# First pair's scores placed around the last group's values, and weight steps placed behind the pairs'

## The chip, the cores and the metric

The kernel runs on one core of a Trainium2 chip. That core has a matrix engine (TensorE, PE in the profile, with its weight loads shown apart as PEld), three element-wise engines (VectorE = DVE, ScalarE = ACT, GpSimd = POOL) and a sync engine (SP), which here issues nearly all transfers between HBM and the on-chip memory (SBUF). Products land in PSUM. Each engine takes its instructions in the order in which they were written and waits on semaphores for the others. The metric is the device time of one execution in microseconds, the median of several runs.

## What is computed

Three layers follow each other: attention over chunks of 32 queries with a local window and 8 memory keys, a gated two-layer network, and a second network with a softmax-like gate and a normalisation.

```python
# attention: B, H, S, D = 4, 8, 768, 64; per chunk of 32 queries a window of 56 keys and 8 memory keys
scores = scale * q_c @ k_full.T;  a = softmax(scores);  out_c = a @ v_full
# x: 3072 tokens x 512
a = x @ w_a;  b = x @ w_b                 # 512 -> 1536
x2 = (a * b) @ w_out                      # 1536 -> 512
h = x2 @ w_in;  solu = h * softmax(h)     # 512 -> 1024
out = (layernorm(solu) * g_ln) @ w_out2   # 1024 -> 512
```

The products are made in a 32-bit format that is rounded on writing, so each operand is kept as a high and a low part, and each product is three matrix products (low by high, high by low, high by high).

## The kernel before, in words

The 3072 tokens are six blocks of 512 tokens. A **group** is 128 queries of one batch entry with all eight heads; four groups make a block. A group passes through the stages P (score bank in PSUM, with masks), S (scores on PE), M (maximum and subtraction on DVE), X (exponential on ACT), N (sums, reciprocal, multiplication), T (transposes on PE, copied back by ACT), V (values on PE, high part cast by ACT) and L (low part on DVE).

Blocks 0 and 1 are done directly: for each of 12 slices f of the 1536 columns, PE makes the products with `w_a` and `w_b` (`ab`, lines 857 to 859, twelve products each, results in the PSUM banks ps0 and ps1, which exist once each); ACT copies the first to the tile G0 (line 1416); DVE multiplies it by the second (`gate`, line 872); ACT and DVE split the result (lines 874 and 878); and `x2_step` multiplies it by `w_out` one slice later. The groups of block 1 run between the products of block 0. A table gives the slot of the loop in which each of their stages is called. The last two of them, called i and j in the code, run after the loop of block 0, beside the first half of block 1's first slice.

The loop of block 1 is cut into 72 ticks, six per slice: half of the first product, the rest, half of the second, the rest, and two halves of the `x2_step` of the slice before. A table says what is called after each tick (`at(t, fn, ...)`); the call puts instructions at the end of the queues of PE, DVE, ACT and SP, whose order is the written one. Two kinds of work are placed there:

- **Pairs.** The groups of blocks 2 to 5 go through the stages two at a time (`pair_P` to `pair_V`, lines 296 to 373). During block 1 four pairs run, d = 4 to 7, one in each 16 ticks. Their queries and keys (640 KB per group) and values (512 KB per group) are loaded into the three buffers of the pool `ld`, in turn; a load waits until the buffer's reader three loads earlier is done.
- **Weight steps.** Blocks 2 to 5 use sums of weight quarters. For each slice q: `s1_whole` (DVE, line 488), `s1_sums` (four DVE operations, line 502), `s1_hi` (a cast on ACT, line 513, into one buffer h, the last third of the tile Z), and `s1_lo` (DVE, line 520); `s1_hi` and `s1_lo` each issue two stores of 256 KB (lines 507 and 508). There is one h: the cast of slice q+1 waits until the stores of slice q have read it. `wo_keep` of slice f issues two stores of 256 KB (line 474), a DVE sum (line 479) and one more store (line 480) of 256 KB.

The cast, the exponential and the copy after a transpose (`pair_T`, line 346) are all in ACT's one queue. The transposed scores stand in the tile EB, which `pair_V` (line 361) reads.

Of the kernel before, what the change touches and what calls it, by code (L numbers as in the profile page):

```python
# [48 lines left out]
NDIR = 2  # L49
# [6 lines left out]
def fused_kernel(  # L56
# [224 lines left out]

    def pair_load(d, i, values):

# [3 lines left out]
        if values:  # L287
            t = ld_tile(n - k, "v")
            nc.sync.dma_start(t, qkv[qi, :, k:n])
            quads[qi]["v"] = t.rearrange("k (c p d) -> k c p d", c=NCH, p=NP)  # L290
        else:
            t = ld_tile(k, "qk")
            nc.sync.dma_start(t, qkv[qi, :, 0:k])
            quads[qi] = dict(
                q=t[:, 0:q].rearrange("d (p t) -> d p t", p=NP),
                k=t[:, q:k].rearrange("d (p t) -> d p t", p=NP),
            )
# [13 lines left out]

    def pair_S(d):

        for i in range(2):
            qi = 2 * d + i
# [976 lines left out]
    for qi, at in zip(qs, (  # L1292
        (24, 24, "8a", "8a", "9b", 31, 32, 32),
        ("8a", 27, "9b", "9b", 31, 33, 34, 34),
# [19 lines left out]
    for f in range(NF1):  # L1314
# [25 lines left out]
        pend = (0, f, gh, gl)  # L1340
        run_slot()
    x2_step(*pend)
    i, j = qs[2:]
# [13 lines left out]
    att_L(i)  # L1357
    T(j)
    V(j)
    att_L(j)  # L1360

# [16 lines left out]
    def pair(d, places):  # L1378
        p, s, m, x, n, t, v = places
        for k, fn in zip(places, (pair_P, pair_S, pair_M, pair_X, pair_N, pair_T, pair_V)):  # L1380
            at(k, fn, d)
            if fn is pair_S:
# [6 lines left out]

    d0 = 2 * NDIR  # L1390
    for j in range(4):
        pair(d0 + j, [16 * j + k for k in (-2 if j else 0, 0, 1, 2, 3, 8, 10)])
    for n in ((0, False), (1, False), (0, True)):
        pair_load(d0, *n)
    for t, fn, i in ((41, x1_hi, 0), (44, x1_lo, 0), (46, x1_hi, 1), (48, x1_lo, 1)):
        at(t, fn, i)
    for q in range(NF1):
        for k, fn in zip(
            ((0, 2, 5, 7), (7, 8, 10, 12), (13, 14, 16, 19))[q % 3], (s1_whole, s1_sums, s1_hi, s1_lo)
        ):  # L1400
            at(16 * (q // 3) + k + 1, fn, q)
    for t, fn, i in (
# [5 lines left out]
    for f in range(NF1):  # L1408
        at((0, 0, 14, 14, 14, 32, 32, 44, 48, 52, 56, 60)[f], wo_keep, f)
    pend = None  # L1410
# [53 lines left out]
    for p, (a, b, c, d, e) in enumerate((  # L1464
# [420 lines left out]
```

## Time and profile before

| | |
|---|---|
| time, median of 3 runs | 889.62 us (889.38 to 890.72) |
| profiled execution: its time / its span | 891.03 us / 889.2 us |
| PE busy / DVE busy / ACT busy, share of the span | 97% / 81% / 45% |
| busy time of the DMA engines, queue of SP | 69.3% |

The span is the time from the first to the last recorded instruction; 1.8 us of the profiled execution lie around it. In a listing by time a row gives the start, the busy time, the engine, the line, the operation with output and inputs, and in brackets the idle time of that engine just before it and what ended it. [...]

### The profile page before, as it was taken

What the parts mean: (1) busy time and instruction counts of PE and PEld (TensorE: products, weight loads), DVE (VectorE), ACT (ScalarE), POOL (GpSimd) and SP (SyncE); (2) the same over time, 40 slices, a digit from 0 to 9 for tenths busy, and PEclk for the clock granted to TensorE, in tenths of its full rate; (3) what the DMA queues carried; (4) which work ended last, traced back from release to release, by engine and by line L of the source; (5) the groups of instructions that cost most, each with busy time, mean ns of one, the idle gap of its engine ahead of it and who ended that gap; (6) DMA issues with size and microseconds to landing.
All of it is one profiled execution on the core that took longest, in us unless ns stands there. A gap on an engine that the chain in (4) does not pass through costs nothing.

```text
span 889.2 us, 16756 instructions
## 1 busy us (share of the span) xinstructions
PE 860.2 (97%) x6696; PEld 709.9 (80%) x6696; DVE 717.3 (81%) x1162; ACT 398.1 (45%) x587; POOL 61.5 (7%) x77
## 2 busy tenths in 40 slices
PE   3899999999999999999999999999999999999998
PEld 3788877787888887888888888878888788888886
DVE  6999965978876675767967778998589999888882
ACT  3677643433343423334645544357254444444432
POOL 0000000000000000000000000000322223222110
PEclk9999999999999999999999999999999999999999
DMA  9995446987699888882798988558903555554353
GB/s 369 422 413 205 154 149 197 303 282 241 215 342 408 310 318 288 322 310 76 252 336 324 342 318 330 203 192 291 332 26 95 166 164 179 160 168 124 119 153 121
DMA packets 103215, 216.08 MB, mean 243 GB/s; under 512 B 8544, under 2 KB 64096, under 8 KB 97888
## 3 DMA queue, kind: packets, MB, share of 16 engines
q1 hardware_dynamic: 103104, 214.99, 69.3%
q8 instruction: 53, 0.87, 0.4%
q14 instruction: 26, 0.21, 0.1%
q0 software_dynamic: 32, 0.00, 0.0%
HBM read 147.85 MB, written 67.11 MB: 242 GB/s over the span
## 4 chain that ended last, share of the span: by engine, by line
PE 68%; DVE 15%; DMA 7%; issue 5%; ACT 2%; SPq 1%; POOL 1%; POOLq 0%; ACTq 0%; DVEq 0%
PE acc L756 24%; PE pab L1185 8%; PE acc L970 8%; PE pab L727 7%; PE acc L727 5%; PE pab L857 2%; PE pab L858 2%; PE pab L859 2%; DVE Z L407 2%; DVE Z L399 2%; PE px L361 2%; PE s L194 2%; PE px L259 1%; DMA r<-ztd 1%; PE acc L857 1%
## 5 line engine op out<-in xcount | busy, mean ns | idle before, releaser
L756 PE MATMUL acc<-w 128*128 128x512 f32 x978 | 227.5, 391 | 0.2 <-DMA w<-wsa 0.2
L756 PEld LDWEIGHTS acc<-w 128*128 128x128 f32 x978 | 182.8, 188 | 38.6 <-DMA w<-wsa 0.6
L1185 PE MATMUL pab<-w 128*128 128x512 f32 (+1 forms) x600 | 134.4, 381 | 1.1 <-ACT w L1157 1.1
L1185 PEld LDWEIGHTS pab<-w 128*128 128x128 f32 x600 | 109.4, 188 | 23.0 <-ACT w L1157 1.5
L857 PE MATMUL pab<-x,w 128*128 128x512 f32 (+1 forms) x200 | 79.2, 396 | 0.9 <-ACT x L273 0.9
L858 PE MATMUL pab<-x,w 128*128 128x512 f32 (+1 forms) x200 | 77.6, 388 | 0.1
L859 PE MATMUL pab<-x,w 128*128 128x512 f32 (+1 forms) x200 | 77.3, 387 | 0.0
L918 POOL TENSOR_TENSOR w2ld<-w2ld 128x256 f32<-128x256 f32 x44 | 37.9, 881 | 545.3 <-ACT r L747 497.1
L727 PE MATMUL pab<-w 128*128 128x512 f32 x288 | 70.3, 391 | 0.3 <-DMA w<-wos 0.3
L769 DVE TENSOR_TENSOR part<-acc,part 128x512 f32<-128x512 f32 x56 | 38.6, 689 | 34.8 <-PE acc L756 28.0
L727 PEld LDWEIGHTS pab<-w 128*128 128x128 f32 x288 | 53.7, 188 | 12.0 <-ACT w L698 0.7
L970 PE MATMUL acc<-w,hx 128*128 128x512 f32 x252 | 60.9, 391 | 1.4 <-ACT part L982 1.3
L970 PE MATMUL acc<-w 128*128 128x512 f32 x252 | 60.6, 391 | 0.1
L970 PEld LDWEIGHTS acc<-w,hx 128*128 128x128 f32 x252 | 47.1, 188 | 11.9 <-ACT part L982 1.7
L970 PEld LDWEIGHTS acc<-w 128*128 128x128 f32 x252 | 47.1, 188 | 10.2 <-ACT part L982 0.5
L727 PE MATMUL acc<-w 128*128 128x512 f32 x216 | 51.9, 390 | 0.1
L727 PEld LDWEIGHTS acc<-w 128*128 128x128 f32 x216 | 40.5, 188 | 8.8 <-ACT w L829 0.4
L857 PEld LDWEIGHTS pab<-x,w 128*128 128x128 f32 x200 | 38.4, 192 | 9.1 <-ACT x L273 1.2
L859 PEld LDWEIGHTS pab<-x,w 128*128 128x128 f32 x200 | 38.4, 192 | 7.5
L858 PEld LDWEIGHTS pab<-x,w 128*128 128x128 f32 x200 | 38.4, 192 | 7.4 <-DVE x L278 0.4
L702 DVE TENSOR_TENSOR w<-r,w 128x512 fp32r<-128x512 f32 x56 | 37.7, 688 | 1.9 <-ACT w L698 1.9
L857 PE MATMUL acc<-gh,w 128*128 128x512 f32 x96 | 38.1, 397 | 0.0
(236 smaller groups left out, 1403.6 us busy)
## 6 DMA issues: line engine op xcount, KB each, us to landing
w<-wsa SPq DMA_DIRECT2D x24, 1024.0 KB, 6.9
w<-wsb SPq DMA_DIRECT2D x24, 768.0 KB, 6.2
raw<-w1d_dram SPq DMA_DIRECT2D x11, 1536.0 KB, 21.7
qk<-qkv_dram SPq DMA_DIRECT2D x20, 640.0 KB, 6.3
w<-wos SPq DMA_DIRECT2D x48, 256.0 KB, 4.5
ztd<-r SPq DMA_DIRECT2D x84, 128.0 KB, 2.5
r<-ztd SPq DMA_DIRECT2D x21, 512.0 KB, 4.0
v<-qkv_dram SPq DMA_DIRECT2D x20, 512.0 KB, 4.9
```

The costliest lines, as they stand in the source:

```text
L194: nc.tensor.matmul(s[CQ * c:CQ * c + CQ, r, p, lo:hi], st["q"][rows, p, CQ * c:CQ * c + CQ], st["k"][rows, p, k0 + lo:k0 + hi], start=True ...
L361: nc.tensor.matmul(px[half:half + 64, r, p // 2, i, t], v[rows, c, p, :], at[rows, p, t], start=True, stop=True,)
L702: nc.vector.tensor_tensor(out=c[:, 1], in0=op_src(k), in1=c[:, 0].bitcast(F32), op=ALU.subtract)
L727: nc.tensor.matmul(ps, w[:, u, sl], g[:, v], start=first and n == 0, stop=last and n == 2, skip_group_check=True,)
L756: nc.tensor.matmul(ps, w[:, u, k], xx[v][:, k], start=(start and k == 0 and i == 0), stop=(stop and k == 1 and i == 2), skip_group_check=True,
L769: nc.vector.tensor_tensor(out=o, in0=a, in1=b, op=op)
L857: nc.tensor.matmul(ps, wl, xh, start=first, stop=False)
L858: nc.tensor.matmul(ps, wh, xl, start=False, stop=False)
L859: nc.tensor.matmul(ps, wh, xh, start=False, stop=last)
L918: (nc.gpsimd if j else nc.vector).tensor_tensor(out=s4[:, i], in0=a, in1=b, op=op)
L970: nc.tensor.matmul(ps, x, y, start=(start and k == 0 and i == 0), stop=(stop and k == 1 and i == 2), skip_group_check=True,)
L1185: nc.tensor.matmul(po, s[x][:, f], wo2(f)[:, h, sl], start=(m == 0), stop=(m == 3 * NF2 - 1))
```

## The change

**The first pair.** Queries and keys of pair d = 4 (groups 8 and 9) no longer go to the pool `ld` but to the two buffers that held block 0's input (`x_tile(0)` and `x_tile(1)`), and their loads are written straight after the loop of block 0. `pair_P` and the scores of group 8 are written between the transposes and the values of group j, the scores of group 9 behind those values. The rest of the pair moves: M from tick 1 to 0, X from 2 to 0, N from 3 to 4, T from 8 to 10, V from 10 to 12.

**A transpose in block 0.** T of block 1's first group is called at slot "10a" and not at 31, so that ACT's copy of its result (line 237) stands ahead of the cast of the gated product (line 874) and not behind it. PE's order there stays.

**The weight steps.** `s1_whole`, `s1_sums`, `s1_hi`, `s1_lo` of slice 0 go from ticks 1, 3, 6, 8 to 3, 9, 10, 11; of slice 1 from 8, 9, 11, 13 to 11, 12, 13, 14; of slice 6 (ticks 33, 35, 38, 40) `s1_hi` goes to 40 and `s1_lo` to 41; the other slices keep theirs. `wo_keep` of slices 0, 1 and 2 goes from ticks 0, 0, 14 to 10, 12, 15. In the stage behind block 1 one of the steps on `w_out` is done and stored two to three places later.

```diff
-    def pair_load(d, i, values):
+    def pair_load(d, i, values, qk=None):
...
-            t = ld_tile(k, "qk")
+            t = ld_tile(k, "qk") if qk is None else qk.rearrange("d k t -> d (k t)")[:, 0:k]
...
-    def pair_S(d):
-        for i in range(2):
+    def pair_S(d, of=(0, 1)):
+        for i in of:
...
-        (24, 24, "8a", "8a", "9b", 31, 32, 32),
+        (24, 24, "8a", "8a", "9b", "10a", 32, 32),
...
+    d0 = 2 * NDIR
+    for n in range(2):
+        pair_load(d0, n, False, x_tile(n, F32, "qk"))
     x2_step(*pend)
...
     T(j)
+    pair_P(d0)
+    pair_S(d0, (0,))
     V(j)
+    pair_S(d0, (1,))
     att_L(j)
...
+            if k is None:
+                continue
...
+    at(3, s1_whole, 0)
     for j in range(4):
-        pair(d0 + j, [16 * j + k for k in (-2 if j else 0, 0, 1, 2, 3, 8, 10)])
-    for n in ((0, False), (1, False), (0, True)):
-        pair_load(d0, *n)
+        pair(d0 + j, [16 * j + k for k in (-2, 0, 1, 2, 3, 8, 10)] if j else (None, None, 0, 0, 4, 10, 12))
+    pair_load(d0, 0, True)
+    pair_load(d0, 1, True)
+    pair_load(d0 + 1, 0, False)
...
-            ((0, 2, 5, 7), (7, 8, 10, 12), (13, 14, 16, 19))[q % 3], (s1_whole, s1_sums, s1_hi, s1_lo)
-        ):
-            at(16 * (q // 3) + k + 1, fn, q)
+        ticks = ((1, 3, 6, 8), (8, 9, 11, 13), (14, 15, 17, 20))[q % 3]
+        if q < 2:
+            ticks = ((3, 9, 10, 11), (11, 12, 13, 14))[q]
+        elif q == 6:
+            ticks = (1, 3, 8, 9)
+        for k, fn in zip(ticks, (s1_whole, s1_sums, s1_hi, s1_lo)):
+            if k > 3 or q:
+                at(16 * (q // 3) + k, fn, q)
...
-        at((0, 0, 14, 14, 14, 32, 32, 44, 48, 52, 56, 60)[f], wo_keep, f)
+        at((10, 12, 15, 14, 14, 32, 32, 44, 48, 52, 56, 60)[f], wo_keep, f)
...
-        ((5, 1), (6, 5), (7, 0), (7, 3), (7, 5)),
+        ((5, 1), (6, 5), (7, 0), (7, 5), (8, 0)),
```

On PE, between the last groups of block 1 and its first slice, the order changes like this (L259 is `att_V`, L235 `att_T`, L194 the scores, L857 to L859 the three products; a row of the program may be two in the trace):

```order
 L259 MATMUL px<-AT,v 64x32 x32
 L235 MATMUL pt<-ident,EB 128x128 x4
+L194 MATMUL s<-qk 32x64 x32
 L259 MATMUL px<-AT,v 64x32 x32
-L857 MATMUL pab<-x,w 128x256
-L858 MATMUL pab<-x,w 128x256
-L859 MATMUL pab<-x,w 128x256
-L857 MATMUL pab<-x,w 128x256
-L858 MATMUL pab<-x,w 128x256
-L859 MATMUL pab<-x,w 128x256
-L194 MATMUL s<-qk 32x64 x64
```

The pair's 64 scores, which stood behind six products of the first slice, stand as two halves of 32 on either side of the last values.

On ACT, from the first exponential of the pair to the copy of its values, before (L1416 copies ps0 to G0, L329 is the exponential, L874 the cast of the gated product, L513 `s1_hi`, L346 the copy after T, L372 the copy after V):

```order
L1416 COPY G_147<-pab 128x512
L329 ACTIVATE EB<-s 128x2x8x64
L874 CAST gh<-G_147 128x512
L513 CAST Z<-Z 128x1024
L1416 COPY G_147<-pab 128x512
L346 COPY EB<-pt 128x1024
L874 CAST gh<-G_147 128x512
L372 COPY xs<-px 128x2x2x256
```

and with the change (L1429 is the copy to G0 now):

```order
L329 ACTIVATE EB<-s 128x2x8x64
L1429 COPY G_147<-pab 128x512
L874 CAST gh<-G_147 128x512
L1429 COPY G_147<-pab 128x512
L874 CAST gh<-G_147 128x512
L346 COPY EB<-pt 128x1024
L513 CAST Z<-Z 128x1024
L372 COPY xs<-px 128x2x2x256
```

The exponential has gone ahead of the first copy to G0, and the cast of slice 0 behind the copy of the transposed scores. At the third pair, d = 6, the cast of slice 6 goes behind L874 and L346 in the same way. At the second pair, d = 5, nothing moves: the cast of slice 3 stays ahead of L346.

On SP, from the load of pair 5's first queries (L293) on, before (L474 and L480 are the stores of `wo_keep`, L507 and L508 those of `s1_hi` and `s1_lo`, L289 loads values):

```order
L293 DMA qk<-qkv_dram 128x1280
L474 DMA wod_94<-w 128x2x256 x2
L480 DMA woz_106<-wz 128x512
L474 DMA wod_95<-w 128x2x256 x2
L480 DMA woz_107<-wz 128x512
L507 DMA wsa_70<-Z 128x2x256
L508 DMA wsb_82<-Z 128x2x256
L507 DMA wsa_70<-Z 128x2x256
L508 DMA wsb_82<-Z 128x2x256
L293 DMA qk<-qkv_dram 128x1280
L289 DMA v<-qkv_dram 128x1024
```

and with the change:

```order
L293 DMA qk<-qkv_dram 128x1280
L507 DMA wsa_70<-Z 128x2x256
L508 DMA wsb_82<-Z 128x2x256
L474 DMA wod_94<-w 128x2x256 x2
L480 DMA woz_106<-wz 128x512
L507 DMA wsa_70<-Z 128x2x256
L508 DMA wsb_82<-Z 128x2x256
L293 DMA qk<-qkv_dram 128x1280
L289 DMA v<-qkv_dram 128x1024
L474 DMA wod_95<-w 128x2x256 x2
L480 DMA woz_107<-wz 128x512
```

The six stores of `wo_keep` of slices 0 and 1 have gone behind the first stores of slice 0's sums; the stores of slices 1 and 2 (`wsa_71`, `wsa_72` and so on) follow after them as before.

## Rows read from the trace of the kernel before

**Rows 1.** Listing by time, PE: values of block 1's first group.

```profile
126.55 1.14 PE L259 MATMUL px<-AT,v 64*64 64x32 f32 x64 [0.81 <-ACT AT L237]
```

**Rows 2.** Listing by time, PE: last values, first slice, pair scores; last row a later pair.

```profile
148.25 0.79 PE L259 MATMUL px<-AT,v 64*64 64x32 f32 x40 [0.73 <-ACT AT L237]
149.43 0.55 PE L259 MATMUL px<-AT,v 64*64 64x32 f32 x24 [0.39 <-issue]
...
150.90 0.39 PE L858 MATMUL pab<-x,w 128*128 128x256 f32 x1
...
152.01 2.10 PE L194 MATMUL s<-qk 64*32 64x64 f32 x128
...
156.55 0.40 PE L857 MATMUL pab<-x,w 128*128 128x512 f32 x1
...
175.91 1.47 PE L194 MATMUL s<-qk 64*32 64x64 f32 x128
```

**Rows 3.** Stretches: busy time of the five engines, PE's granted clock, DMA share, GB/s.

```profile
152.00:153.00 1.00, 1.00 (x75) 0.99 (x78) 0.38 (x1) 0.00 (x0) 0.00 (x0) 0.50 0.85 336
```

**Rows 4.** Listing by time, DVE and ACT, the pair's maximum and exponential.

```profile
151.09 1.28 DVE L479 TENSOR_TENSOR wz<-w 128x512 f32<-128x512 f32 x2
...
154.19 1.22 DVE L322 TENSOR_REDUCE mx<-s 128x16 f32<-128x1024 f32 x1 [1.81 <-PE s L194]
...
155.32 0.59 ACT L1416 COPY G<-pab 128x512 f32<-128x512 f32 x1 [4.65 <-PE pab L859]
...
156.71 1.03 ACT L329 ACTIVATE EB<-s 128x1024 f32<-128x1024 f32 x1 [0.80 <-DVE s L323]
```

**Rows 5.** Listing by time, PE: transposes and values of pair 4.

```profile
161.43 1.06 PE L345 MATMUL pt<-ident,EB 128*128 128x128 f32 x8 [0.61 <-DVE EB L337]
...
165.53 2.07 PE L361 MATMUL px<-EB,v 64*64 64x32 f32 x128 [0.29 <-ACT EB L346]
```

**Rows 6.** Listing by time: load of group j's queries and keys, and their first use.

```profile
134.97 0.34 SPq L154 DMA_DIRECT2D qk<-qkv_dram  x1
...
141.50 0.86 PE L194 MATMUL s<-qk 64*32 64x64 f32 x64
```

**Rows 7.** Listing by time, SP: stores of `wo_keep` 1 (last), slice 0, slice 2.

```profile
158.00 1.08 SPq L480 DMA_DIRECT2D woz<-wz  x1
164.11 0.36 SPq L507 DMA_DIRECT2D wsa<-Z  x1
...
182.41 0.48 SPq L508 DMA_DIRECT2D wsb<-Z  x1
```

**Rows 8.** Stretches, columns as in Rows 3.

```profile
160.00:161.00 1.00, 0.82 (x4) 0.36 (x2) 0.97 (x2) 0.00 (x0) 0.00 (x0) 1.00 1.07 389
163.00:165.00 2.00, 2.00 (x10) 1.50 (x8) 1.49 (x2) 1.97 (x3) 0.00 (x0) 1.00 0.02 7
165.00:189.00 24.00, 23.71 (x349) 19.69 (x348) 21.64 (x33) 7.88 (x12) 0.00 (x0) 1.00 0.97 321
```

**Rows 9.** Transfers, KB each, us from issue to landing: of Rows 6's load, Rows 7's last.

```profile
qk<-qkv_dram SPq DMA_DIRECT2D x1, 640.0 KB, 3.9
...
wsb<-Z SPq DMA_DIRECT2D x1, 256.0 KB, 6.4
```

**Rows 10.** Listing by time, ACT and PE: cast of slice 3, copy and values of pair 5.

```profile
188.94 1.05 ACT L513 CAST Z<-Z 128x1024 fp32r<-128x1024 f32 x1 [0.55 <-DMA wsb<-Z]
189.89 1.01 ACT L346 COPY EB<-pt 128x1024 f32<-128x1024 f32 x1
...
192.06 2.07 PE L361 MATMUL px<-EB,v 64*64 64x32 f32 x128
```

**Rows 11.** The same at pair 6: cast of slice 6, values.

```profile
217.13 1.05 ACT L513 CAST Z<-Z 128x1024 fp32r<-128x1024 f32 x1 [5.57 <-DMA wsb<-Z]
...
219.66 2.07 PE L361 MATMUL px<-EB,v 64*64 64x32 f32 x128 [1.02 <-ACT EB L346]
```

**Rows 12.** Listing by time, PE, the values of a group early in the span.

```profile
26.28 1.93 PE L259 MATMUL px<-AT,qkv 64*64 64x32 f32 x64 [0.73 <-ACT AT L237]
```

More of the change, by code (lines that the diff above doesn't have):

```diff
@@ L1388, in pair @@
                 at(k, pair_load, d + 1, 0, True)
-    d0 = 2 * NDIR
+    at(3, s1_whole, 0)
     for j in range(4):
-        pair(d0 + j, [16 * j + k for k in (-2 if j else 0, 0, 1, 2, 3, 8, 10)])
-    for n in ((0, False), (1, False), (0, True)):
-        pair_load(d0, *n)
+        pair(d0 + j, [16 * j + k for k in (-2, 0, 1, 2, 3, 8, 10)] if j else (None, None, 0, 0, 4, 10, 12))
+    pair_load(d0, 0, True)
+    pair_load(d0, 1, True)
+    pair_load(d0 + 1, 0, False)
     for t, fn, i in ((41, x1_hi, 0), (44, x1_lo, 0), (46, x1_hi, 1), (48, x1_lo, 1)):
@@ L1397, in fused_kernel @@
     for q in range(NF1):
-        for k, fn in zip(
-            ((0, 2, 5, 7), (7, 8, 10, 12), (13, 14, 16, 19))[q % 3], (s1_whole, s1_sums, s1_hi, s1_lo)
-        ):
-            at(16 * (q // 3) + k + 1, fn, q)
+        ticks = ((1, 3, 6, 8), (8, 9, 11, 13), (14, 15, 17, 20))[q % 3]
[6 more added lines that the diff above has]
+                at(16 * (q // 3) + k, fn, q)
     for t, fn, i in (
```

## The prediction

> **What bounds the kernel now.** PE works nearly the whole span (97% in the table), so I looked for the places where PE stands still or runs slowly, and then for what sets the time of the stretch behind. First the listing of PE between the two blocks. The values of block 1's first group wait 0.81 us for ACT's copy of the transposed scores [rows 1]. From 147.5 to 156.5 us there are more holes [rows 2]: the last group's values wait 0.73 us for the same copy, stand for 0.39 us with no cause in the profile, and end at 149.98 (149.43 + 0.55); the first slice gets going only at 150.90, behind the cast and subtraction of those values; then the pair's scores take 2.10 us where a later pair's take 1.47. [...] The pair's transposes and values wait again, 0.61 us on DVE and 0.29 us on ACT [rows 5].
>
> Next the transfers. The six stores of `wo_keep` 0 and 1 are issued up to 158.00; at 163 to 165 us the DMA engines stand at 2%; slice 0's first store is issued at 164.11 [rows 7, 8]. From 165 to 189 us the DMA engines are 97% busy at 321 GB/s [rows 8]: nearly full for 24 us. At its end the last store of slice 2's high part, issued at 182.41, needs 6.4 us to land [rows 7, 9], at 188.81, and ACT's cast of slice 3 has waited for exactly that (0.55 us) when it starts at 188.94. Behind the cast in ACT's queue is the copy for pair 5, and PE takes up that pair's values at 192.06, without waiting [rows 10]. So here a chain store, cast, copy, values runs some 1.1 us ahead of PE (the copy ends at 190.90). At pair 6 the same chain has overtaken PE: the cast waits 5.57 us for a store and the values wait 1.02 us [rows 11].
>
> **The change part by part.** Times are those of the profiled execution (span 889.2 us, 891.03 us with what lies around it); it is 1.4 us above the median of 889.62, so I carry the difference over to the median.
>
> *The copy in block 0* goes ahead of the cast. PE had made the transposes long before, so the 0.81 us should go whole. 0 to 0.8, taken 0.8.
>
> *The scores around the last values.* They do the same work at another place. One half (0.74 us, half of 1.47) fills the 0.73 us wait for the copy, the other the 0.92 us (149.98 to 150.90) until the first slice has its low part. Before, it is 6.57 us from the end of the values to the first product of the second slice (149.98 to 156.55). Now PE could be there after 0.92 us and 23 products of 256 columns. 18 of them took at most 2.4 us behind the scores (154.11 to 156.55), so 23 take about 3.1, and PE would be ready 4.0 us after the values. It is not let in: ps0 has to be copied first, and on ACT that copy now stands behind the exponential. DVE is free for the maximum 1.11 us after the values (its next operation before was at 151.09), from the start of the maximum to the exponential it is 2.52 us (154.19 to 156.71), the exponential takes 1.03 and the copy 0.59 [rows 4]: 5.25 us. So a new wait of some 1.2 us stands there, and the gain is 6.57 - 5.25 = 1.3 us; 0.9 at worst, 1.9 if the 0.39 us hole goes too. That cover also hides a low clock in the first slice, if it comes again.
>
> *The two waits of the pair* (0.61 and 0.29): 12 more products of 0.24 us are put ahead of the transposes ((161.43 - 0.61 - 156.55) / 18 products = 0.237 each), and the normalisation moves by one tick only. 0 to 0.9, taken 0.9. PE would then come to pair 5's values 0.8 + 1.3 + 0.9 = 3.0 us earlier, at 189.1.
>
> *The loads of the pair's queries and keys* are issued ahead of group j's own 640 KB, which now are last of three. Theirs took 3.9 us from 134.97, landing at 138.9, 2.6 us before use at 141.50 [rows 6, 9]. Two more loads are 1.31 MB, 4.0 us at the 331 GB/s worked out below, less what they are issued earlier. 0 to 1.4 us late, taken 0; I put it into the bounds of the next step.
>
> *The weight steps behind the pair.* Slice 0's cast now stands behind the pair's copy, and on SP the six stores of `wo_keep` 0 and 1 stand behind slice 0's first stores. They lose the time in which the DMA engines were free and join the full stretch. Slice 0's store is issued after: end of the values 149.98 - 0.8, the 5.25, 30 products of 0.237 (12 of each weight and half an `x2_step`), transposes 1.06, copy 1.01, cast 1.05 [rows 5, 10] = 164.7, 0.6 us later than before. Ahead of slice 2's store there are 6 x 262,144 bytes = 1.57 MB more; at 321 GB/s / 0.97 = 331 GB/s that is 4.75 us, less the free 3% of 24 us, 0.7. Sum: lands 4.6 us later. Lower bound: the hole of 0.39 gone (0.2 us later), 389 GB/s as in the best second [rows 8] (4.0 us) and twice the free time: 2.8. Upper: keys late by 0.4, no free time: 5.8. I take 4.2, near the rate of the long stretch, since 24 us are better evidence than one second of it. Landing 193.0, cast 193.1, copy 0.95 behind it (188.94 to 189.89) at 194.1, values 1.07 later: 195.1. Against 192.06 that is **3.1 us later**, and PE, ready at 189.1, has stood still for most of 6 us. What PE won before is all inside that wait.
>
> [...]
>
> *Slice 6's cast behind pair 6's copy.* The 1.02 us wait goes, since the copy no longer stands behind a cast that waits for a store. 0.7 to 1.0, taken 1.0.
>
> *The clock.* Before, holes of 0.4 to 0.9 us among small products end in a stretch at 0.50 [rows 2, 3]. A wait of 6 us should do so too. Half clock costs 64 small products 1.93 us [rows 12] where 40 and 24 took 0.79 and 0.55, so pair 5's 128 take up to 3.86 against 2.07, 1.8 us more. Part of a slow stretch passes in the wait. 0 to 1.8, taken 0.6.
>
> [...]
>
> *The step on `w_out`* moves by two or three places behind PE's own work, where no PE wait of over 0.3 us stands near: 0.
>
> Sum: 3.1 - 1.0 + 0.6 = **+2.7 us**: span 891.9, median 892.3.
>
> **The rivals.**
> - *It drains faster.* If the full stretch can run at 389 GB/s and no slow clock follows, the landing is 2.8 late, the values at 193.8, +1.7, and with the 1.0 of pair 6 +0.7: 890.3. For it: single seconds reach 389. Against: 24 us at 97% and 331.
> - *The keys come late.* If the three loads take the full 1.4 us too long, the scores of j, and with them slice 0's store, move by that: 893.7.
> - *The change only gains.* If slice 2's store has landed by 187.0, 1.8 us earlier than before (the point from which pair 5's copy is ready when PE is), the wait does not exist and 3.0 + 1.0 us are won: 885.6. For it: the DMA engines move the same bytes in all. Against: they are free earlier for some 8 us that the change doesn't use.
> - *The slow clock in full*: 893.5, a part of the forecast's own range.
>
> **How the numbers follow.** Chances: the store holds pair 5's values as summed 0.60 (own range 891.0 to 895.0; 0.2 of it with the clock in full), drains faster 0.20, keys late 0.06, only gains 0.14. The likeliest gives 892.3. A difference of 0.2% (1.8 us) is about what a measurement of this kernel can tell from no change. Slower by more: most of the first and the third, 0.59. Within: the rest of the first and most of the second, 0.25. Faster: the last and the second's best end, 0.16. The range 888.0 to 895.0 leaves out the last case and the top of the first.
>
> **What would show it.** Right: the two halves of the scores without a wait, the scores near 0.74 us each; a wait of PE of about 1 us before the second slice, ended by ACT; DMA engines idle from about 154 to 164 us and full from there to 193; ACT's slice 3 cast waiting several us for `wsb`; PE's longest wait behind block 0 at pair 5's values, and a clock under 1.00 there; no wait at pair 6's. Wrong: pair 5's values without a wait, or slice 2's store landing within 6 us of 182; then the rate or the free time of the transfers was misjudged.

## The result and the profile after

The changed kernel takes 899.16 us (897.71 to 900.43, four runs) against 889.5 us of the kernel before on the same chip: ratio 1.0097, 95% interval 1.008 to 1.0113. It is 9.7 us slower; the forecast was 2.7 us slower, with a range that ended at 895.0. The direction held, the size did not.

The profiled execution of the changed kernel has a span of 895.9 us, 6.7 us more than before. It lies 1.45 us below the median of its runs, and that of the kernel before (891.03) 1.5 us above the 889.5; together these are the 3.0 us between 6.7 and 9.7. From the end of block 1 on, both traces run alike: at the first of line 756's products into the tile `acc` the changed kernel is 6.8 us behind (279.6 against 272.8). So all of it happens before 272 us: 0.8 us are won at 125 us, and the loss comes behind 146 us.

PE by time (start, busy time, line, output and inputs, shape, count; in brackets the idle time before and what ended it):

```profile
125.77 1.14 PE L259 MATMUL px<-AT,v 64*64 64x32 f32 x64
...
146.67 0.66 PE L194 MATMUL s<-qk 64*32 64x64 f32 x40
148.46 0.43 PE L194 MATMUL s<-qk 64*32 64x64 f32 x24 [1.13 <-issue]
148.82 1.14 PE L259 MATMUL px<-AT,v 64*64 64x32 f32 x64
149.88 0.66 PE L194 MATMUL s<-qk 64*32 64x64 f32 x40
152.56 0.43 PE L194 MATMUL s<-qk 64*32 64x64 f32 x24 [2.02 <-issue]
...
157.23 0.64 PE L857 MATMUL pab<-x,w 128*128 128x512 f32 x1
...
164.34 1.03 PE L345 MATMUL pt<-ident,EB 128*128 128x128 f32 x8
168.03 2.07 PE L361 MATMUL px<-EB,v 64*64 64x32 f32 x128
175.70 0.86 PE L194 MATMUL s<-qk 64*32 64x64 f32 x64
178.03 0.84 PE L194 MATMUL s<-qk 64*32 64x64 f32 x64 [1.47 <-DMA qk<-qkv_dram]
...
197.79 3.06 PE L361 MATMUL px<-EB,v 64*64 64x32 f32 x128 [4.06 <-ACT EB L346]
209.72 1.46 PE L194 MATMUL s<-qk 64*32 64x48 f32 x128
...
225.88 2.07 PE L361 MATMUL px<-EB,v 64*64 64x32 f32 x128
```

- The 0.81 us of [rows 1] is gone: 125.77 without a wait.
- The two halves of the scores, meant for the holes of [rows 2], bring holes of their own: each half stops after 40 of its 64 products, for 1.13 and 2.02 us, and the profile names no cause ("issue"). The second slice starts at 157.23, later than the 156.55 of [rows 2].
- At the scores of pair 5 PE is 0.21 us ahead of the kernel before (175.70 against 175.91), not 3.0. There it waits 1.47 us for keys, which it never did before.
- Pair 5's values wait 4.06 us and start at 197.79 against 192.06 in [rows 10]. They take 3.06 us in place of 2.07, and pair 6's scores come 11.93 us after them where it was 10.39 (202.45 - 192.06): 1.54 us more, with no wait in between, at a clock that stands at 0.50 for part of that time (below). Pair 6's values wait no longer, as in [rows 11] they did.

In the kernel before, the load of pair 5's second queries and keys on SP, and pair 6's scores on PE:

```profile
166.73 0.35 SPq L293 DMA_DIRECT2D qk<-qkv_dram  x1
...
202.45 1.47 PE L194 MATMUL s<-qk 64*32 64x48 f32 x128
```

The changed kernel on ACT and SP: slice 3's cast and the copy behind it; slice 0's first store, the load of pair 5's second queries and keys, slice 2's last store.

```profile
195.78 1.04 ACT L513 CAST Z<-Z 128x1024 fp32r<-128x1024 f32 x1 [3.11 <-DMA wsb<-Z]
196.73 1.01 ACT L346 COPY EB<-pt 128x1024 f32<-128x1024 f32 x1
```
```profile
167.40 0.38 SPq L507 DMA_DIRECT2D wsa<-Z  x1
...
172.27 0.45 SPq L293 DMA_DIRECT2D qk<-qkv_dram  x1
...
188.91 0.46 SPq L508 DMA_DIRECT2D wsb<-Z  x1
```

Slice 0's store goes out at 167.40 where I had 164.7, and slice 2's store lands some 2.7 us later than forecast (the cast behind it at 195.78; forecast 193.1). Stretches of the changed kernel (PE, PEld, DVE, ACT, POOL busy, clock, share of the DMA engines, GB/s):

```profile
154.00:168.00 14.00, 14.00 (x68) 11.93 (x66) 10.84 (x17) 5.30 (x7) 0.00 (x0) 0.88 0.00 1
168.00:196.00 28.00, 24.26 (x349) 19.71 (x348) 21.54 (x32) 6.78 (x10) 0.00 (x0) 1.00 1.01 337
...
199.00:200.00 1.00, 1.00 (x48) 1.00 (x45) 0.93 (x3) 0.00 (x0) 0.00 (x0) 0.50 1.04 342
```

The DMA engines are empty for 14 us (share 0.00) and then full for 28 (1.01), and behind PE's wait the clock stands at 0.50.

### The profile page after: what moved, and what is told of

It is laid out like the page before. It is cut to its first block, busy times and chain, and to the rows that moved or that the text cites. A ratio compares the mean times of both kernels' runs of the same rounds, so it can differ in the third digit from the quotient of the medians.

```text
span 895.9 us, 16755 instructions
## 1 busy us (share of the span) xinstructions
PE 862.4 (96%) x6696; PEld 711.6 (79%) x6696; DVE 717.7 (80%) x1162; ACT 398.0 (44%) x587; POOL 61.5 (7%) x77
## 4 chain that ended last, share of the span: by engine, by line
PE 75%; DVE 10%; DMA 6%; issue 4%; ACT 2%; SPq 1%; POOL 1%; POOLq 0%; ACTq 0%; DVEq 0%
PE acc L756 23%; PE pab L1185 9%; PE acc L970 9%; PE pab L727 7%; PE acc L727 5%; PE pab L857 4%; PE pab L858 4%; PE pab L859 4%; DMA wsb<-Z 2%; PE acc L857 2%; PE acc L859 2%; PE acc L858 2%; PE px L361 1%; PE s L194 1%; PE px L259 1%
## 5 line engine op out<-in xcount | busy, mean ns | idle before, releaser
L857 PE MATMUL pab<-x,w 128*128 128x512 f32 (+1 forms) x200 | 80.1, 400 | 0.5 <-ACT x L273 0.5
L859 PE MATMUL pab<-x,w 128*128 128x512 f32 (+1 forms) x200 | 77.8, 389 | 0.0
L857 PEld LDWEIGHTS pab<-x,w 128*128 128x128 f32 x200 | 39.0, 195 | 9.1 <-ACT x L273 0.6
L859 PEld LDWEIGHTS pab<-x,w 128*128 128x128 f32 x200 | 39.0, 195 | 7.5
L858 PEld LDWEIGHTS pab<-x,w 128*128 128x128 f32 x200 | 39.0, 195 | 7.1 <-DVE x L278 0.2
L857 PE MATMUL acc<-gh,w 128*128 128x512 f32 x96 | 38.1, 397 | 0.0
```

The costliest lines, as they stand in the source:

```text
L857: nc.tensor.matmul(ps, wl, xh, start=first, stop=False)
L858: nc.tensor.matmul(ps, wh, xl, start=False, stop=False)
L859: nc.tensor.matmul(ps, wh, xh, start=False, stop=last)
```

## The experiments

Two questions: what stops PE among the scores, and how much of the loss comes from the scores and how much from the weight steps. The table has all runs: the median, the ratio to the kernel before on the same chip with its 95% interval, and from the profiled execution the stalls marked "issue" among the last groups' and the pair's small products, and the start of pair 5's values with the wait before it. The two single executions have no interval.

| run | median us | ratio (interval) | stalls us | pair 5's values, wait |
|---|---|---|---|---|
| changed kernel | 899.16 | 1.0097 (1.0080 to 1.0113) | 1.13 + 2.02 | 197.79, 4.06 |
| weights_back | 892.21 | 1.0025 (1.0011 to 1.0039) | 0.83 + 1.47 | 192.44, 0 |
| copy_slice6 | 889.00 | 0.9986 (0.9973 to 0.9998) | 0.43 | 191.70, 0 |
| weights_only | 893.47 | 1.0042 (1.0028 to 1.0056) | 0 | 195.35, 1.76 |
| shift32 | 898.64 (1 run) | | 0.47 | 196.59, 4.10 |
| quiet | 900.26 | 1.0112 (1.0093 to 1.0131) | 1.10 + 2.02 | 197.55, 3.68 |
| ticks_back | 897.34 | 1.0082 (1.0064 to 1.0099) | 1.10 + 1.47 | 198.18, 1.74 |
| wb_quiet | 889.53 | 0.9991 (0.9980 to 1.0002) | 1.75 | 191.45, 0 |
| wb_half | 891.82 | 1.0018 (1.0007 to 1.0030) | 0.83 | 192.73, 0 |
| wbq_exp_later | 890.68 | 0.9993 (0.9979 to 1.0007) | 1.98 | 192.02, 0 |
| wbq_exp_shift | 890.84 | 1.0000 (0.9986 to 1.0015) | 0.47 | 191.39, 0.55 |
| weights_back2 | 890.03 (1 run) | | 1.13 + 1.75 | 192.97, 0 |
| after_again | 899.56 | 1.0097 (1.0080 to 1.0114) | 0.82 + 1.75 | 197.23, 3.53 |
| after_shift | 898.66 | 1.0086 (1.0070 to 1.0102) | 0.75 | 195.27, 3.70 |
| cs6_keys_early | 890.16 | 0.9997 (0.9987 to 1.0007) | 0 | 191.34, 0 |

### What stops PE: shift32, wb_half

From the first hole to the second PE runs 24 + 64 + 40 = 128 products and as many weight loads, 256 instructions. The page of the changed kernel has a queue for instructions:

```profile
PE 862.4 (96%) x6696; PEld 711.6 (79%) x6696; DVE 717.7 (80%) x1162; ACT 398.0 (44%) x587; POOL 61.5 (7%) x77
...
q8 instruction: 53, 0.87, 0.4%
```

53 packets for 2 x 6696 = 13,392 PE instructions are 253 each. The theory: PE's instructions come in packets of 256 over the DMA engines, and PE stands when it has used one up before the next is there.

**shift32** puts 32 more products ahead.

```diff
     T(0)
+    shift = ps_ab.tile([P, TB], F32, tag="ps1", name="shift")
+    for _ in range(16):
+        nc.tensor.matmul(shift[0:32, 0:64], ident[0:64, 0:32], ident[0:64, 0:64], start=True, stop=True)
     att_M(1)
```

> The changed kernel with 16 more products of 32 by 64 between the first group's transposes and the third group's scores, where PE stands for over 4 us; they write to a bank that nothing reads. Each is two loads and two products in the trace, so 64 instructions more ahead of all that follows. Theory (PE's instructions come in packets of 256, and the stall is the wait for the next packet): the stalls come 32 of 64 products sooner, after 8 in the first half of the pair's scores and after 8 in the second half, and no longer after 40; in sum about 3 us as before. Rival (a wait for data, a semaphore or a bank that the profile does not show at that product): both stay after 40 of 64.

PE of shift32 by time:

```profile
148.12 0.86 PE L194 MATMUL s<-qk 64*32 64x64 f32 x64
148.92 1.14 PE L259 MATMUL px<-AT,v 64*64 64x32 f32 x64
149.99 0.32 PE L194 MATMUL s<-qk 64*32 64x64 f32 x8
150.78 0.79 PE L194 MATMUL s<-qk 64*32 64x64 f32 x56 [0.47 <-issue]
```

The stall has moved by exactly 32 products, from 40 to 8. No product's data or bank has changed, so the rival falls. The count from the start of the execution says the same. Up to the stall, the tables of stretches have these products of PE (the first count in brackets), in the kernel before up to its hole of 0.39 us, in the changed kernel up to either stall, and in shift32:

```profile
0.00:149.40 149.40, 131.07 (x1488) 107.57 (x1489) 125.47 (x150) 85.79 (x97) 3.53 (x9) 1.00 0.73 276
```
```profile
0.00:148.40 148.40, 130.74 (x1488) 107.23 (x1489) 125.33 (x150) 85.75 (x97) 3.53 (x9) 1.00 0.76 286
0.00:152.50 152.50, 132.82 (x1616) 109.02 (x1616) 126.09 (x152) 86.39 (x99) 3.53 (x9) 1.00 0.75 283
```
```profile
0.00:150.70 150.70, 136.08 (x1616) 111.90 (x1616) 125.77 (x151) 86.37 (x99) 3.53 (x9) 1.00 0.75 283
```

Whatever product stands there, PE stops behind the 1488th or the 1616th, 128 apart. My second number was wrong: the stall of the first half is gone and the sum is 0.47 us, not 3. So how long PE stands depends on the place of the stop: 1.13 and 2.02 us after 40 of the 64 products, 0.47 us after 8.

The packets can be seen on the DMA engines. In the changed kernel the one tenth of a microsecond from 146.10, and in shift32 the one from 148.30, hold one each (queue, packets, MB, share):

```profile
q8 instruction: 1, 0.02, 58.3%
```
```profile
q8 instruction: 1, 0.02, 57.4%
```

The stalls end 2.3 us and 2.4 us after them (148.46 and 150.78). The twenty stalls of this place in all the profiles show 2.2 to 2.9 us from the packet to PE's next product. 128 small products took only 1.47 to 2.10 us in [rows 2, 5]. Where both stalls occur (six profiles), 3.55 to 4.10 us pass from the end of the first to the end of the second, in the changed kernel 4.10 (148.46 to 152.56): that is what the 128 small products between them cost.

**wb_half** asks for the opposite: not the packet moved, but larger products in between (on top of weights_back, below).

```diff
     V(j)
-    pair_S(d0, (1,))
     att_L(j)
...
+    at(0, pair_S, d0, (1,))
```

> weights_back with the second half of the pair's scores behind the first six products of block 1's first slice and not ahead of them. Theory (PE uses 256 instructions in the time of 128 small products, 1.5 to 2.1 us, faster than the next packet comes; large products in between give it time): the first stall stays near 1 us, the second falls from 1.5 us to under 0.6, and the kernel is 0.5 to 1.5 us faster than weights_back. Rival (the stall belongs to these products, by their data or bank): the second half stalls as long as before wherever it stands.

PE of wb_half by time, the second half of the scores and the start of the second slice:

```profile
151.38 1.06 PE L194 MATMUL s<-qk 64*32 64x64 f32 x64
156.69 0.80 PE L857 MATMUL pab<-x,w 128*128 128x512 f32 x1 [1.91 <-ACT G L1425]
```

The second half runs through behind six products of 256 columns, so the stall is not these products' own. The time is the same as weights_back's (1.0018 against 1.0025) and not 0.5 to 1.5 us better: the wait for the copy to G0 grew from 1.16 to 1.91 us and took the gain.

### What the scores cost and what the weight steps cost

Three kernels share the copy in block 0 and slice 6's step, and add one of the two large parts or none.

**copy_slice6**: the kernel before with `"10a"` for the first group's T and ticks 1, 3, 8, 9 for slice 6.

> The kernel before with two parts of the change alone: the transposes of block 1's first group called at slot 10a, and slice 6's cast and low part behind pair 6's copy. Theory: the two waits of 0.81 and 1.02 us go and nothing takes their place, so 1.8 us faster, 887.8. Rival: PE's 0.8 us are only waited for later (at the last group's values, the cast behind them, or pair 5's copy behind slice 3's cast): 1.0 us or less, 888.6 and above.

**weights_back**: the changed kernel with the weight steps put back.

```diff
-    at(3, s1_whole, 0)
...
-        if q < 2:
-            ticks = ((3, 9, 10, 11), (11, 12, 13, 14))[q]
-        elif q == 6:
+        if q == 6:
...
-        at((10, 12, 15, 14, 14, 32, 32, 44, 48, 52, 56, 60)[f], wo_keep, f)
+        at((0, 0, 14, 14, 14, 32, 32, 44, 48, 52, 56, 60)[f], wo_keep, f)
```

> The changed kernel with the weight steps of slices 0 and 1 and `wo_keep` of slices 0 to 2 at the places they had before (ticks 1, 3, 6, 8; 8, 9, 11, 13; and 0, 0, 14); the pair's scores, its loads, the copy in block 0 and slice 6 stay as changed. Theory: the scores cost as much by PE's two stalls (3.15 us in the changed kernel's trace) as all else in that stretch wins, so PE is 0.2 us ahead of the kernel before at pair 5's scores; the stores are early again, pair 5's keys land in time, its values start at about 191.9 us without a wait, and slice 6's step gives 1.0 us: 1.2 us faster than before, near 888.4, with both stalls still there. Rival A, the prediction's own sum without the weight steps: 3.0 and 1.0 us won, 885.6. Rival B, the keys in the other buffers or the later ticks of the pair hold the rest up and the weight steps do not: values still near 197.8 us and 897 to 899.

**weights_only**: copy_slice6 with these weight steps at the changed places.

> The kernel before with the copy in block 0, slice 6's step, and the weight steps of slices 0 and 1 and of `wo_keep` 0 to 2 at the changed places; the first pair's scores, loads and ticks stay as before. Theory: no new stall among the small products, so slice 0's first store goes out at about 164 us and not at 167.4; the full stretch then ends some 4.2 us later than before, pair 5's values start near 195 us behind slice 3's cast, and a low clock follows them: 892 to 894. Rival A: the weight steps alone cost what the whole change cost, values near 197.8 us and 897 or more. Rival B: they cost nothing without the scores, 887.8 as with the two small parts alone.

ACT (cast of slice 3) and PE (values of pair 5) of weights_only by time:

```profile
193.35 1.04 ACT L513 CAST Z<-Z 128x1024 fp32r<-128x1024 f32 x1 [0.81 <-DMA wsb<-Z]
...
195.35 2.07 PE L361 MATMUL px<-EB,v 64*64 64x32 f32 x128 [1.76 <-ACT EB L346]
```

copy_slice6 is 1.2 us faster than before (0.14% of 890), where the theory had 1.8 and the rival 1.0 or less. Both waits are gone in its trace, but of the 0.8 us from block 0 only 0.36 are left at pair 5's values (191.70 against 192.06): its clock still stands at 0.50 at 155 us, where the kernel before is back at 1.00. It is the only kernel here whose whole interval lies below 1, by a hair, and so the best version that came out of this. For weights_only the forecast was met in part by luck: slice 0's first store goes out at 167.60 and not at about 164, and the low clock that should follow the wait does not come (the values take 2.07 us). Beside copy_slice6, in the same series, the scores' move costs 3.2 us (892.21 - 889.00) and the weight steps 4.5 us (893.47 - 889.00). With the 1.2 us these give 6.5 us slower than before; the changed kernel is 8.6 us slower (0.97% of 890). The two parts together may cost some 2 us more than each for itself, but each interval is over a microsecond wide either way.

For weights_back the theory's 888.4 and rival A's 885.6 were too low, rival B's 897 to 899 too high. Its profiled execution (889.57) was the fastest of its twelve and shows the stalls and only 0.74 us loss against copy_slice6 at pair 5's values. It also shows a third stall, which the table's column leaves out, PE by time:

```profile
174.98 1.47 PE L194 MATMUL s<-qk 64*32 64x64 f32 x128
...
178.69 0.50 PE L859 MATMUL acc<-gh,w 128*128 128x512 f32 x1 [0.89 <-issue]
```

It stands behind the next run of small products, pair 5's scores. 1999 products of PE are recorded ahead of it, which is the 1616 and three packets of 128, less one. In spite of the first two stalls PE is still 0.58 us ahead of copy_slice6 at these scores (174.98 against 175.56); the loss comes behind them. weights_back2, wb_quiet and wbq_exp_later have it too (0.95, 0.75, 0.86 us). Why the packet comes too late there (176.4 us, in the kernel before 173.3) no run shows. A second profile was meant to find the other 2 us.

> The same kernel as weights_back, for a second profile: the profiled run of the first was its fastest (889.57 against a median of 892.21, up to 895.70). Theory (the stalls vary with the moment at which a packet gets its turn on the DMA engines): in a slower run the stalls among the scores or at later small products are longer by most of the difference in time. Rival (the difference lies in another stretch, such as the stores that hold pair 5's copy): stalls of 2.3 us in sum as in the first profile.

It came out at 890.03, with the first two stalls 2.88 us in sum against 2.30 and pair 5's values 0.53 us later than in the first. That is in line with the theory, but no execution as slow as the median was caught, so where the other 2 us of weights_back lie stays open.

### Does other traffic delay the packet: quiet, wb_quiet

The change of **quiet** is `at(2, pair_load, ...)` for the three loads behind the scores.

> The changed kernel with the three loads behind the scores (values of groups 8 and 9, queries and keys of group 10, 1.66 MB) issued at tick 2 of block 1 instead of ahead of tick 0, so that the DMA engines have little to do while PE runs its small products; they fall in the time from 154 to 167 us in which the engines stood idle. Theory (PE stands because its next packet of 256 instructions comes late, and the packet shares the DMA engines with these loads): the two stalls of 1.13 and 2.02 us, 3.15 in sum, fall below 1.5 us in sum. Rival A (the packet takes its time whatever else is moved): sum unchanged, 2.8 to 3.5 us. For the whole: the values of pair 5 are held by slice 2's store, so at most 2 us faster than the changed kernel, 896 to 899.

It tested nothing: nothing stands ahead of these loads on SP that waits, so they went out as early as before (the third at 149.87; in the changed kernel 150.04). It is the changed kernel a second time, with stalls of 1.10 and 2.02 us. In **wb_quiet** the stores of `wo_keep` stand ahead of the loads and hold them back to 156.57.

> The changed kernel with the weight steps of slices 0 and 1 and `wo_keep` at their places of before (the run weights_back) and the three loads at tick 2 as well. There PE's own work sets the time of the stretch, so what the stalls among the scores give back shows whole. Theory (packets late behind the loads): stalls below 1.5 us in sum and 1 to 2 us faster than weights_back (892.2), near 890.5. Rival (packet time fixed): no difference.

The packets come 1.1 to 1.2 us sooner (the two at 144.4 and 148.3, in weights_back 145.6 and 149.4), the first stall is gone, the second is 1.75 us. The second packet has only followed the first: PE goes on behind the 1488th product at 147.1 us and behind the 1616th at 150.96, 3.8 us later; in weights_back at 148.14 and 151.69, 3.55 us later. In sum the stalls are 1.75 in place of 2.30, not below 1.5 as expected, but the kernel is faster: 0.9991 against 1.0025, intervals apart. So the loads have a part in the delay of the first packet, and 1.75 us of stall are left with the loads out of the way. That the 2.7 us between the medians come from the packets is not shown: the profiled executions take the same time (889.51 and 889.57).

### Can the scores' move be mended: wbq_exp_later, wbq_exp_shift, cs6_keys_early

**wbq_exp_later** is wb_quiet with `(None, None, 0, 1, 4, 10, 12)` for the first pair's ticks; **wbq_exp_shift** also does 16 products of an earlier group twice.

```diff
-        for p in range(NP):
+        for p in (0, 1, 0, 1, 2, 3) if qi == 5 else range(NP):
```

> wb_quiet (scores around the last values, weight steps at their places of before, three loads at tick 2) with the pair's exponential at tick 1 and not 0, so that on ACT the first copy to G0 stands ahead of it as it did before the change. In wb_quiet PE waits 1.16 us for that copy ahead of the second slice. Theory: that wait goes and nothing else moves up to pair 5, so 1.1 us faster than wb_quiet: 888.4. Rival: the exponential then comes later, and the normalisation, the transposes or slice 0's steps take the 1.1 us back: within 0.4 us of 889.5.

> wbq_exp_later with 16 products of the scores of block 1's second group done twice (the same values again; 32 products more in the trace, 0.4 us of PE's time), so that the ends of the packets of 256 instructions fall 32 small products sooner, as in shift32, from which a stall of 0.47 us was left. In wb_quiet the second half of the pair's scores stalls 1.75 us after 40 of 64. Theory: it comes after 8 of 64 and is under 0.7 us; with the 0.4 us paid that is 0.7 us faster than wbq_exp_later, 887.7. Rival: the sum of the stalls stays whatever the place, and the kernel is 0.4 us slower than wbq_exp_later.

The first took the wait away and won nothing: the stall came out at 1.98 us, the clock stood at 0.50 from 152 to 155 us, where wb_quiet has 1.00, and the second slice started at 156.06 (wb_quiet: 155.62). The second put the stall where it was forecast, after 8 of 64, and PE came to the second slice 2.6 us sooner. PE of wbq_exp_shift by time:

```profile
149.78 0.79 PE L194 MATMUL s<-qk 64*32 64x64 f32 x56 [0.47 <-issue]
...
153.48 0.40 PE L857 MATMUL pab<-x,w 128*128 128x512 f32 x1
...
161.29 1.09 PE L345 MATMUL pt<-ident,EB 128*128 128x128 f32 x8 [0.81 <-DVE EB L337]
165.72 2.07 PE L361 MATMUL px<-EB,v 64*64 64x32 f32 x128 [0.59 <-ACT EB L346]
...
175.28 0.84 PE L194 MATMUL s<-qk 64*32 64x64 f32 x64 [1.04 <-DMA qk<-qkv_dram]
...
191.39 2.07 PE L361 MATMUL px<-EB,v 64*64 64x32 f32 x128 [0.55 <-ACT EB L346]
```

It is at pair 5's values only 0.63 us sooner (191.39 against 192.02): the pair's normalisation, its copy and pair 5's keys now come last, one after the other. Of the 2.6 us that PE has gained up to the second slice they leave those 0.63. The median is 890.84, that of wbq_exp_later 890.68: not the 0.7 us gain of the theory.

**cs6_keys_early** keeps the scores where they were and takes only the early loads of the keys, with the three other loads at tick 2.

> copy_slice6 (the kernel before with the copy in block 0 and slice 6's step) and the keys of the first pair loaded early into the buffers of block 0's input, the values of groups 8 and 9 and the keys of group 10 at tick 2 behind `wo_keep`'s stores; the scores stay behind the first six products. Theory: less is moved while PE runs the small products of the last groups, so the stall of 0.43 us at the last values goes, and at best part of the slow clock in the first slice (0.6 us): 0.4 to 1.0 us faster than copy_slice6, 888.0 to 888.6. Rival: the hole is closed by the wait for the cast behind it, no difference to copy_slice6.

PE of cs6_keys_early by time, the last values, the pair's scores and its transposes:

```profile
147.83 1.14 PE L259 MATMUL px<-AT,v 64*64 64x32 f32 x64 [0.73 <-ACT AT L237]
...
150.68 1.48 PE L194 MATMUL s<-qk 64*32 64x64 f32 x128
...
160.70 1.06 PE L345 MATMUL pt<-ident,EB 128*128 128x128 f32 x8 [1.31 <-DVE EB L337]
```

The stall is gone and the pair's scores take 1.48 us where [rows 2] have 2.10, yet the transposes wait 1.31 us for the normalisation. There is no gain on copy_slice6 (0.9997 against 0.9986).

### What holds pair 5: ticks_back, after_shift, after_again

**ticks_back** is the changed kernel with T and V of the first pair at ticks 8 and 10.

> The changed kernel with transposes and values of the first pair at ticks 8 and 10 as before, not 10 and 12. By that the loads of pair 5's second queries and keys and of its first values (1.15 MB), which wait for the buffers that these values free, stand ahead of slice 0's and slice 1's stores on SP again. Theory (in the changed kernel these loads went out at 172.3 us in place of 166.7, into the full stretch, and cost the 1.47 us wait for pair 5's keys and some 2.4 us of the later slice 2 store): no wait for the keys, pair 5's values near 195.5 us and not 197.8, 2 to 2.5 us faster than the changed kernel. Rival (the stalls among the scores alone make slice 2's store later than predicted): pair 5's values within 0.7 us of 197.8, no gain.

SP of ticks_back (slice 0's first store), and its PE (scores and values of pair 5), by time:

```profile
170.17 0.38 SPq L507 DMA_DIRECT2D wsa<-Z  x1
```
```profile
176.80 1.47 PE L194 MATMUL s<-qk 64*32 64x64 f32 x128 [0.30 <-ACT s L307]
...
198.18 2.07 PE L361 MATMUL px<-EB,v 64*64 64x32 f32 x128 [1.74 <-ACT EB L346]
```

The keys are in time, as expected, but the values are not earlier. I had missed that slice 0's cast then stands behind the copy of the values on ACT as well: its first store goes out at 170.17, 2.8 us later than in the changed kernel. That the values are only 0.4 us later puts the loads' part at 2.4 us on the other side (an estimate), and weights_only agrees: its first store goes out at 167.60, as in the changed kernel, but the load ahead of it at 164.68 and not behind it at 172.27, and pair 5's values come 2.4 us sooner.

**after_again** and **after_shift** are the changed kernel once more, and with the 32 products ahead as in wbq_exp_shift.

> The changed kernel once more, beside the next one on the same chip: near 899, and its profiled run again some 2 to 3 us below the median of its runs if that gap belongs to this kernel; at the median if it was chance.

> The changed kernel with 16 products of the scores of block 1's second group done twice (the same values; 32 products more in the trace, 0.4 us), so that its stalls come after 8 of 64 and shrink to some 0.5 us, as in shift32 and wbq_exp_shift. Theory A (the time held back by slice 2's store decides, and the stalls only through slice 0's first store): the values of pair 5 at most 1.5 us earlier than the changed kernel's, 0 to 1.5 us faster. Theory B (the timed executions are slower than the profiled ones because the stalls are longer in them): its median falls to its profiled run, near 897, 2 to 3 us faster than the changed kernel. Rival C: nothing moves, within 0.5 us of the changed kernel.

With the stalls at 0.75 us in sum slice 0's store goes out 2.1 us sooner (165.26) and the values start 2.5 us sooner (195.27) than in the changed kernel's first profile, 2.0 sooner than in after_again; theory A allowed 1.5. The wait is still 3.70 us. The median falls by 0.9 us against after_again, inside theory A; the intervals overlap. Its profiled execution (896.19) lies 2.5 us below its median, that of after_again (899.30) at it, so a gap between profiled and timed executions is no mark of this kernel. What differs between two executions of the changed kernel is in part the clock behind the wait: in after_again pair 6's scores start 13.03 us after pair 5's values, 2.64 us more than before. PE of after_again by time:

```profile
197.23 3.64 PE L361 MATMUL px<-EB,v 64*64 64x32 f32 x128 [3.53 <-ACT EB L346]
210.26 1.46 PE L194 MATMUL s<-qk 64*32 64x48 f32 x128
```

## Why the prediction was wrong, step by step

- **The copy in block 0**: right. The wait of 0.81 us went whole.
- **The scores around the last values**: this is the step that failed. That one half fills the 0.73 us wait and the other the 0.92 us took it that PE can run 64 + 4 + 64 + 64 + 64 small products in a row. It stops twice, 128 products apart, for 1.13 and 2.02 us; by the theory above a packet of its instructions ends at both places. The values end at 149.96 and not at 149.18, and 7.27 us pass from there to the second slice (157.23 - 149.96) in place of 5.25: longer by just the 2.02 us of the second stall (in after_again 6.98, with a second stall of 1.75). The row that warned stood in the prediction, the hole of 0.39 us with no cause after 40 of 64 products [rows 2]. I counted it among what could only get better. The new wait of 1.2 us for the copy to G0 was right in after_again (1.16 us); in the first profile, where the clock stands at 0.50 from 155 to 157 us, the second slice starts without a wait.
- **The two waits of the pair**: right, both are gone; but with the stalls PE is 0.21 us ahead at pair 5's scores and not 3.0.
- **The loads of the pair's keys**: in time in the changed kernel, though not in the three runs with 32 products more, where PE waits 0.46 to 0.50 us for keys just ahead (at 141 to 142 us). But I looked only at the first pair's loads. Pair 5's second keys and its first values, 1.18 MB, wait for the buffers that the first pair's values free; with those at tick 12 they went out at 172.27 and not 166.73, behind slice 0's stores and those of `wo_keep` 0 in the full stretch. That cost 1.47 us at PE and, estimated from ticks_back and weights_only, some 2.4 us at slice 2's store. This term is missing in the sum: the loads belong to the moved step as much as its products.
- **The weight steps**: the mechanism was right in each of its links (engines idle to 168, full to 196; the cast 3.11 us behind `wsb`; pair 5's copy behind the cast; the longest wait of PE behind block 0 there). Its size, 3.1 us at pair 5's values, became 5.7 with the two steps above: slice 0's store, summed to 164.7, went out at 167.40. In weights_only, without them, it was 3.65 us (195.35 - 191.70), and 195.35 against the 195.1 of the sum. That is closer than the sum deserved: in that kernel slice 0's store came 3.9 us later than in copy_slice6 (167.60 against 163.71) where I had 0.6 (with V at tick 10 the cast of slice 0 stands behind the copy of the values on ACT), and part of that time the loads issued at 164.68 filled. How much the 1.57 MB cost by themselves is not shown. That slice 2's stores do not pass what stands ahead of them on SP was an estimate of mine that no run shows; in the changed kernel the cast behind the one issued at 188.91 started at 195.78, 6.87 us later, where it was 6.53 us before (182.41 to 188.94) [rows 7, 10].
- **Slice 6's cast**: right, 1.02 us gone.
- **The clock**: mis-sized. I took 0.6 of a possible 1.8 us; it was 1.54 in the first profile and 2.64 in after_again, the second above my bound. There the values, at 0.50 throughout, took 3.64 us in place of 2.07, and the other 1.07 us went to products behind them, which the bound left out. The 1.93 us of [rows 12] were no sure price for it: the table of stretches has 1.00 there (26 to 28 us). The full 1.8 us would have been nearer for both. In the other runs the price is 1.5, 1.6 and 2.9 us (quiet, after_shift, shift32, with waits of 3.68, 3.70 and 4.10 us) or nothing (ticks_back and weights_only, with waits of 1.74 and 1.76 us).
- **The step on `w_out`**: no wait of its kind appears; 0 stands.

The largest part of the error is the 2.6 us at pair 5's values. Put together for the profiled executions, at these values 3.1 became 5.73, behind them 0.6 became 1.54, at pair 6 -1.0 was -1.05 (7.27 at its scores, 6.22 at its values), and a new wait of 0.49 us came at pair 7's values: 6.7 us.

Of the rivals, "only gains" is refuted by the wait at pair 5. "Drains faster" gave 193.8 for pair 5's values, and they came at 197.79; the full stretch moved 337 GB/s on the mean, close to the 331 of the sum. "The keys come late" had the right mechanism at the wrong pair. "The slow clock in full" adds 1.2 us and so reaches 893.5 only.

## What to carry to other kernels

Count instructions, not only time. Here 128 small products took 1.47 to 2.10 us, and from the end of one stall to the end of the next it was 3.55 to 4.10, so the holes could not be filled with more small products; the sign to look for was a short stall without a cause inside such a run (0.39 us in [rows 2]). When a step is moved, follow the buffers it frees to the loads that wait for them, and those loads to what now stands ahead in the queue. And each part should be measured alone first, above all where the next limit is half a microsecond away: of this change only the two smallest parts gained.

## What the runs showed of the hardware

On the DMA engines the page counts 53 packets of a queue for instructions, 16 KB each (0.87 MB in all), and for PE 13,392 instructions, 253 to a packet; two stalls in a row stand 128 products and their weight loads apart, and 32 products ahead moved the stall by 32 products (shift32). That the 53 are PE's, 256 instructions in each, and that PE stands at a packet's end is read from these numbers. From the packet's appearance on a DMA engine to PE's next product it was 2.2 to 2.9 us in twenty stalls, while 128 small products took 1.47 to 2.10 us in [rows 2, 5] and 128 of 512 columns would take some 30 us (an estimate from the 0.237 each that the prediction works out). With the three loads of 1.7 MB held back the first packet came 1.2 us sooner (144.4 in wb_quiet, 145.6 in weights_back). What sets the moment at which a packet comes, no run shows.

PE's granted clock does not follow such holes alike in every execution: behind the stalls it stands at 0.50 from 155 to 157 us in the changed kernel, where products of 256 columns start 0.21 us apart, while in after_again, with stalls of 0.82 and 1.75 us, they start 0.12 us apart up to 155.43, as they do at 1.00 in the kernel before. Behind the wait at pair 5 it fell to 0.50 in both (199 to 201 us; 197 to 203 us in after_again), at a price of 1.54 and 2.64 us. That may be part of why the six runs of after_again scatter from 897.98 to 901.40 us.
